# A second-level Strassen product in the first place of the last down projection

## The chip, the cores and the metric

The kernel runs on one core of one Trainium2 chip. The metric is the device time of one execution in microseconds. Before the change the three timed runs took 714.13, 714.17 and 714.49 us; the median is 714.17.

The core has a matrix engine (TensorE, PE in the profile; its weight loads are shown as PEld), a vector engine (VectorE, DVE), a scalar engine (ScalarE, ACT), a general engine (GpSimd, POOL) and a queue for transfers (SyncE, SP). Each takes its own instructions in order, and they wait for each other by semaphores. Matrix products are summed in eight banks of PSUM of 128x512 floats.

## The reference

One transformer block on 2048 tokens with 1024 features, in bfloat16: a layer norm, linear attention with a residual, a second layer norm, and a gated feed-forward net with a residual. What the change touches is the net:

```python
h = x + _A_ref(_layernorm(x, axis=-1), A_wqkv, A_wo)
h2 = h + _B_ref(_layernorm(h, axis=-1), B_W_gate, B_W_up, B_W_down)
# _B_ref:
gate = jnp.einsum("bsd,df->bsf", x, W_gate)
up = jnp.einsum("bsd,df->bsf", x, W_up)
gate = gate * (lambda x, dt: x.astype(dt))(gate > 0, gate.dtype)
h = gate * up
return jnp.einsum("bsf,fd->bsd", h, W_down)
```

W_gate and W_up are 1024x3584, W_down is 3584x1024.

## The kernel before

The net is done in two passes of 1024 tokens. Each pass has 14 feed-forward units (`ffn_unit`, L1660; even ones make gate, odd ones up for four blocks of 128 hidden features) and then a down projection (`down_pass`, L1950). This document is about the second pass: its units run from 471 to 633 us, its down projection from 633 to the end.

The down projection of a pass is a matrix product of 1024 tokens x 3584 hidden features with 3584 x 1024 weights. It is done by the Strassen-Winograd scheme: hidden activations and weights are split into 2x2 blocks, and seven products of blocks or of sums of blocks take the place of eight. The seven are numbered 0 to 6. A product in the **direct** form (`direct`, L2076) is 56 matmuls with 512 columns: 14 pairs of hidden blocks times four groups of 128 tokens, weights brought in five chunks (`WCH`). A product in the **second-level** form (`level2`, L2102) applies the same scheme once more within the product: seven smaller products M1, M7, M6, M2, M5, M4, M3 (in this order) of 14 matmuls with 256 columns each. Each M takes one 448 KB weight operand from the ring `wdring` and one operand of activations. Four of the seven activation operands are sums (`l2_sums`, L1905, on VectorE, L1908), called sg here, one for each of M7, M5, M6 and M3; the other three are quarters of the block. Of the weight operands, too, four are sums.

In the second pass before the change, product 0 is direct and products 1 to 6 are second-level (`L2SET`, L692). A product of the second level uses four banks, `a, f, b, c`: M1 into a, copied by ScalarE into b (a fork, L850); M7 into f; M6 adds to b, which is forked into c; M2 adds to a; M5 adds to c; M4 adds to b; M3 adds to c. So M3 may not start before M5 has been read out of c. Products use the banks 0 to 3 and 4 to 7 in turn.

When an M has been summed, its bank is read into the float buffers U and V or into the output tiles, a quarter at a time (`q_add`, L2004, a VectorE addition from PSUM, 128x512). `ev` adds into U or V; `ev_out` makes an output tile of 128x512 and adds it to the output in memory by a transfer from GpSimd (L1977); M7 is read twice, the others once for each target. Product 4 serves two targets. Product 0 before the change is copied out of PSUM by ScalarE twice: into U (`e_s1`) and, later, into Wf in the tensor RH (`e_w`, L1987), since product 1 adds to U while product 2 needs the first product alone.

The order of VectorE's work in a down pass is written by hand: `at(p, i, f)` puts f behind the i-th unit of product p (L2174 on), and i counts chunks of a direct product or the M's in the order above, from 0. There go the sums sg for the products ahead, D2 (`d2`, L2066; the difference of D1 and a block, an operand of product 1) and D4 (`d4`, L2070; an operand of product 6), each in two instructions of 128x3584. GpSimd adds the residual h of one output block to U (`add_h`, L1994) behind product 3, from a tile that SyncE loads (`ld_h`, L1958).

The weight operands are made once. Those of product 2 are made in the second pass: in each pair of units a raw piece is loaded (`load_xr`, L736), stored to memory as it is, and VectorE makes four differences of 128x256 that are stored too (`x_wsums`, L741). Those of products 1, 3, 4, 5, 6 are made in the first pass (`wl_sums`, L801), where for one of them GpSimd does the subtractions (`addw`, L823 and 824), each of them tied to TensorE's latest instruction and called from `mid`, a list that `ffn_unit` takes from at fixed places (L1817, 1825, 1869, 1880). In the second pass `mid` is empty.

Weights come by a ring of nine buffers in the second pass; the load for a buffer is issued by SyncE as soon as TensorE is done with it.

A unit's products are called P1 to P7, and the M's within P5 and within P1 of the next unit M1 to M7 and R1 to R7; h11, h12, h21, h22 are the four quarters of its result, and c12, c22 and s5a are VectorE's reads out of PSUM (L1707). Behind the last unit `hh_pair` makes D1 and D3.

Of the kernel before, what the change touches and what calls it, by code (L numbers as in the profile page):

```python
# [132 lines left out]
def bass_sequential_preLN__linear_attn_block__glu_gated_reglu__prompt_kernel(  # L133
# [63 lines left out]
    t_v = t_scr.rearrange("p (k o m c) -> p k o m c", k=2, o=8, c=HNW)  # L197
    r_scr = nc.dram_tensor("r_scr", [P, 2 * NPAIR * NW], bf16).ap()
    r_v = r_scr.rearrange("p (s k m c) -> p s k m c", s=2, k=4, c=HNW)
    l_scr = nc.dram_tensor("l_scr", [6 * 4 * P, WDW], f16).ap()  # L200
    l_v = l_scr.rearrange("(o j p) (m c) -> p o j m c", p=P, j=4, c=HNW)
# [3 lines left out]
    with es:  # L205
# [92 lines left out]
        def x2(st):  # L298
# [17 lines left out]
        xr = RW[:, 0:4 * NW].rearrange("p (z k c) -> p z k c", z=2, k=2)  # L316
        lx = RW[:, 4 * NW:8 * NW].bitcast(f16).rearrange("p (z j c) -> p z j c", z=2, j=4)
        xs1 = RX[:, 0:2 * D].bitcast(f16).rearrange("p (j k t) -> p j k t", j=4, k=2)
        g1 = RX[:, 2 * D:4 * D].bitcast(f16).rearrange("p (s j c) -> p s j c", s=2, j=4)
# [5 lines left out]
        sg_g = [RWG[:, x:x + 4 * WDW].bitcast(f16).rearrange("p (j m t) -> p j m t", j=4, t=SHB)  # L325
                for x in (0, NWX * NDC * 2 * P)]
        XSZ = KH * S // 2

# [78 lines left out]
        sl_xw = slots("dxw_", 2)  # L407
        sl_lx = slots("dlx_", 2)
        sl_out = slots("dout_", NOS)
        sl_out2 = slots("dou2_", STB)  # L410
# [72 lines left out]
        B_lx = [bufs("lx%d_" % i, 4) for i in range(2)]  # L483
        B_rscr = [bufs("rscr%d_" % i, NPAIR) for i in range(2)]
        B_hnE = bufs("hnE_", STB)
# [203 lines left out]
        WSRC = [("b", 0, 0), ("t", 1), ("b", 1, 0), ("t", 2), ("t", 0), ("t", 3), ("b", 1, 1)]  # L689
        LIDX = {("t", 0): 0, ("t", 1): 1, ("t", 2): 2, ("t", 3): 3, ("b", 1, 1): 4, ("b", 1, 0): 5}  # L690
        LSRC = [("q", 0, 0), ("s", 2), ("s", 1), ("q", 1, 0), ("s", 0), ("s", 3), ("q", 1, 1)]
        L2SET = [(1, 3, 4, 5, 6), (1, 2, 3, 4, 5, 6)]  # L692
        WLIST = []
        for p2 in range(NPASS):
            for pi, src in enumerate(WSRC):
                if pi in L2SET[p2]:
                    WLIST += [(p2, src, x) for x in LSRC]
                else:
                    WLIST += [(p2, src, c) for c in WCH]
# [11 lines left out]
        def load_wd_next():  # L711
            L = wd_next[0]
            if L >= wd_lim[0]:
                return
            wd_next[0] += 1
            i = wd_slot(L)
            _, src, x = WLIST[L]
            dst = wdring[i]
            if src in LIDX and x[0] in ("s", "q"):
                li = LIDX[src]  # L720
                if x[0] == "s":
                    ap, rd = l_v[:, li, x[1]], B_lscr if li < 4 else B_wscr if li == 4 else B_xscr
                elif li < 4:
                    ap, rd = t_v[:, x[1], 2 * li + x[2]], B_tscr[x[1]::2]
                else:
                    ap, rd = r_v[:, li - 4, 2 * x[1] + x[2]], B_rscr[li - 4][x[1]::2]
                if x[0] == "s" or li < 4:
                    dst = dst.bitcast(f16)
                dma(sl_wd[i], dst.rearrange("p (m c) -> p m c", c=HNW), ap, "ld_wl_%d" % L, reads=rd,
                    writes=[B_wd[i]])  # L730
                return
            q0, q1 = x
            dma(sl_wd[i], dst[:, 0:(q1 - q0) * NW].rearrange("p (q c) -> p q c", c=NW),
                wd_v[:, src[1], q0:q1, src[2] * NW:(src[2] + 1) * NW], "ld_wd_%d" % L, writes=[B_wd[i]])
# [6 lines left out]
        def x_wsums(m):  # L741
# [20 lines left out]
            def two():  # L762
# [3 lines left out]
                load_xr(m + 2)  # L766
            return [one, two]

        def load_wraw(q):
# [889 lines left out]

        def ffn_unit(ps_, n, pre, wina, winb, mid=(), lna=(), lnb=(), tail=()):  # L1660
            Lg = (ps_ * NPAIR + n) * 2
# [164 lines left out]
            else:  # L1826
# [13 lines left out]
                if n == 0:  # L1840
# [6 lines left out]
                dve(ftmp[:, 1, :].rearrange("p (t c) -> p t c", t=2), bank(BE[1]).rearrange("p (t c) -> p t c", t=2),  # L1847
                    m5.unsqueeze(1).to_broadcast([P, 2, SHB]), [B_X, B_s5[0]], [B_s5[1]], "s5a")
                r15()
                p6(1)  # L1850
# [32 lines left out]
            if up:  # L1883
                fin5(1, 1, c22, B_c22, "h22")
                fin5(1, 0, c12, B_c12, "h12")
            else:
# [47 lines left out]

        def sg_hole(t1):
            v = hh16[:, 0:NFT:2, t1 * SBW:(t1 + 1) * SBW]

            def go(j, m0=0, m1=NM):
                b0, c0 = NM * (j // 2), (j % 2) * SHB
                return v[:, b0 + m0:b0 + m1, c0:c0 + SHB], [B_hh[2 * (b0 + m)][t1] for m in range(m0, m1)]  # L1940
            return go

        q_d2 = q_flat(D2, lambda k, m0, m1: [B_D2])
        q_d1 = q_flat(D1, lambda k, m0, m1: [B_D1[2 * m + k] for m in range(m0, m1)])
        q_10, q_11, q_d3, q_d4 = q_hh(1, 0, hh), q_hh(1, 1, hh), q_hh(0, 1, hh16), q_hh(1, 0, hh16)
        sg_ro, sg_rg0, sg_rg2 = sg_plain(sg_o, B_sgo), sg_plain(sg_g[0], B_sgg), sg_plain(sg_g[1], B_sgg)
        sg_x0, sg_x1 = sg_hole(0), sg_hole(1)
        V4 = (ftmp[:, 0:STB], B_U), (ftmp[:, STB:2 * STB], B_V)

        def down_pass(ps_, fill):  # L1950
# [35 lines left out]

            def e_w(j):  # L1987
                ident_act(Wf[:, j], bank(XB[j]), [B_bank[XB[j]]], [B_W[j]], "dsw")

# [112 lines left out]
            def level2(pi, bks, Q, sg, evac, spare=None):  # L2102
# [3 lines left out]
                def prod(mi, bk, x, start):  # L2106
# [3 lines left out]
                    wd_use[0] += 1  # L2110
                    w = wdring[ws]
                    if WSRC[pi][0] == "t" or WLIST[L][2][0] == "s":
                        w = w.bitcast(f16)
# [47 lines left out]
            OS, O2 = (outst, B_outst), (out2, B_out2)  # L2161
            sgs = {1: sg_ro, 2: sg_rg2, 3: sg_x0, 4: sg_ro, 5: sg_rg2 if last else sg_rg0, 6: sg_x1}
            direct(0, XB, a_hh(0, 0), True, e_s1)
            level2(1, YB, q_d2, sgs[1], ev("dU", (U, U)))
            if last:
                level2(2, XB, q_10, sgs[2], ev_out(0, 0, WV, OS, sl_out))
            else:
                direct(2, XB, a_hh(1, 0), False, e_11)
            level2(3, YB, q_d3, sgs[3], ev("dV", (V, U)))
# [21 lines left out]
            hi = (2, 3, 0, 1)  # L2191
            at(0, 0, lambda: d2(0, NH), lambda: d2(NH, NPAIR))
            at(0, 1, sg6[0])
            at(0, 2, *sg6[1:3])
            at(0, 3, sg6[3])
            for i in range(4):
                at(1, 2 + i, sg7[i])
            sg5 = l2_sums(q_d1, sgs[4], "sg5")
            for i in range(4):
                at(2, (1 + i) if not last else 2 + i, sg5[i])  # L2200
            if not last:
                claim(B_sgg, B_w[0:4])
                at(2, 2, lambda: d4(0, NH))
# [3 lines left out]
            else:  # L2207
                claim(B_W, B_hnT)
                at(1, 0, *each(e_w))
                for i in range(4):  # L2210
                    at(3, 2 + i, sg4[i])
                at(2, 0, lambda: ld_h(0, 1))
                at(3, 0, lambda: d4(0, NH))
                at(3, 6, *each(add_h, U, 0, 1, order=hi))
                at(5, 0, lambda: d4(NH, NPAIR))
            for i in range(4):
                at(5, 1 + i, sg3[i])
            for f_, places in fill:
# [278 lines left out]
        for p_ in range(NPASS):  # L2497
            done = []
            for q in range(NPAIR):
# [11 lines left out]
                if p_ == 0:  # L2511
# [25 lines left out]
                    if q == NPAIR - 1:  # L2537
                        for _ in range(NWS - 4):
                            load_wd_next()
                    continue  # L2540
                if q == 0:
                    claim(B_xr + flat(B_lx), B_wd[0:NWS - 3])
                    load_xr(0)
                    load_xr(1)
                if q > 0:
                    winb.append(tq[3])
# [7 lines left out]
                else:  # L2554
                    claim(B_sgg, B_w[2:6])
                    g_ = l2_sums(q_10, sg_rg2, "sg2", 0, NM - 1)
                    winb.append(g_[0])
                if q % 2 == 0:
                    winb.append(w0_)
                ffn_unit(1, q, pre, wina, winb)  # L2560
                if q == NPAIR - 3:
# [3 lines left out]
                if q == NPAIR - 1:  # L2565
                    claim(B_wd[0:NWS - 3], B_xr + flat(B_lx))
                    for _ in range(NWS - 3):
# [11 lines left out]
            else:  # L2579
                claim(B_V, B_xs5 + flat(B_g5))  # L2580
                claim(B_hres + B_ds, B_xs1 + flat(B_g1))
                ge = l2_sums(q_10, sg_rg2, "sg2", NM - 1, NM)
                late = [(g_[1], (0, 3)), (ge[0], (1, 0)), (ge[1], (1, 0)), (g_[2], (1, 1)),
                        (ge[2], (2, 0)), (g_[3], (2, 0)), (ge[3], (2, 0))]
            if p_ + 1 < NPASS:
# [83 lines left out]
```

## Time and profile before

| | us |
|---|---|
| median of three runs | 714.17 |
| the profiled execution | 714.61 |
| its span, first to last instruction | 712.8 |
| TensorE busy | 706.6 |
| VectorE busy | 606.0 |
| ScalarE busy | 411.5 |
| GpSimd busy | 143.1 |
| product 0 of the last down pass (633.04 to 645.12) | 12.08 |
| product 2 of it (655.93 to 666.63) | 10.70 |
| the last weight load on TensorE ends | 709.74 |

The profile is one execution. Engines' times overlap, so what counts is where TensorE has to wait; the chain of work that ended last shows it. In a list of groups or a timeline a line ends with the idle time ahead of the instruction and what ended it, in brackets. TensorE's clock was 1.000 throughout.

### The profile page before, as it was taken

To read this page: it belongs to the slowest core of one execution; us is meant where nothing else is said; L and a number is where in the kernel's file an instruction comes from. 1 tells how busy PE (TensorE), PEld (TensorE's weight loads), DVE (VectorE), ACT (ScalarE), POOL (GpSimd) and SP (SyncE) were. 2 spreads that over 40 slices of the span, in tenths; PEclk is the share of its full clock that TensorE was granted. 3 is DMA by queue.
4 is the path that set the end of the run, shared out by engine and by line. 5 is a ranking of instruction groups with operands and counts; after the bars stand their busy time and mean duration, and the time that the engine had idled before them with its cause. 6 is when DMAs were issued, how large, how long until landed. Compare 5 with 4: busy or idle time off the path is not lost.

```text
span 712.8 us, 13267 instructions
## 1 busy us (share of the span) xinstructions
PE 706.6 (99%) x5039; PEld 391.6 (55%) x5039; DVE 606.0 (85%) x974; ACT 411.5 (58%) x741; POOL 143.1 (20%) x206
## 2 busy tenths in 40 slices
PE   8999999999999999999999999999999999999998
PEld 3344444444444455555554658865555555547887
DVE  6988867899878899999998787888889888988985
ACT  4887666764973687878786411046666767633010
POOL 3231100114982223132312001310000000000331
PEclk9999999999999999999999999999999999999999
DMA  9843244114999799999897989995344544267996
GB/s 297 262 104 77 36 119 164 39 31 95 233 199 287 224 330 290 327 255 297 261 294 239 275 247 319 318 220 159 100 132 114 144 120 125 74 207 256 320 317 187
DMA packets 195104, 144.21 MB, mean 202 GB/s; under 512 B 53984, under 2 KB 172512, under 8 KB 195040
## 3 DMA queue, kind: packets, MB, share of 16 engines
q1 hardware_dynamic: 190048, 138.77, 66.9%
q0 software_dynamic: 4032, 3.67, 3.7%
q10 hardware_dynamic: 960, 0.92, 0.4%
q8 instruction: 40, 0.66, 0.4%
q14 instruction: 24, 0.20, 0.1%
HBM read 98.76 MB, written 32.51 MB: 184 GB/s over the span
## 4 chain that ended last, share of the span: by engine, by line
PE 93%; DMA 2%; DVE 2%; issue 1%; SPq 1%; ACT 0%
PE ps L845 93%; DMA RE<-in_A_x_dram 1%; DMA RAB<-in_A_wqkv_dram 1%; DVE RW L1068 1%; DMA RAB<-RXH 1%; DVE RC L1068 1%; SPq L637 1%; ACT RXH L885 0%; DVE RWG L1093 0%; DVE RE L1968 0%; DVE st L859 0%; DVE RX L1184 0%; DVE RE L1245 0%; DVE RWG L1908 0%; DVE RX L929 0%
## 5 line engine op out<-in xcount | busy, mean ns | idle before, releaser
L850 ACT ACTIVATE ps<-ps 128x512 f32<-128x512 f32 (+1 forms) x263 | 133.1, 517 | 182.2 <-PE ps L845 138.1
L845 PE MATMUL ps<-RC,RO 128*128 128x512 f16 x616 | 147.0, 370 | 0.0
L845 PEld LDWEIGHTS ps<-RC,RO 128*128 128x128 f16 x616 | 59.9, 98 | 53.3 <-ACT ps L850 1.2
L850 ACT ACTIVATE RE<-ps 128x512 f32<-128x512 f32 (+3 forms) x106 | 63.8, 627 | 32.1 <-PE ps L845 18.0
L845 PE MATMUL ps<-RC,RWG 128*128 128x512 f16 x320 | 81.0, 380 | 0.6 <-DVE RC L1068 0.6
L845 PE MATMUL ps<-RH,RWG 128*128 128x512 bf16 (+1 forms) x348 | 77.7, 349 | 0.0
L1977 POOL DMA_DIRECT2D out_dram<-RX x20 | 17.9, 1258 | 271.5 <-DVE RX L1968 218.4
L845 PE MATMUL ps<-RH,RO 128*128 128x512 bf16 (+1 forms) x256 | 65.3, 380 | 0.0
L1707 DVE TENSOR_TENSOR RE<-ps,RE 128x1024 bf16<-128x1024 f32 (+1 forms) x42 | 44.0, 1047 | 18.2 <-PE ps L845 18.1
L845 PE MATMUL ps<-RW,RAB 128*128 128x256 f16 (+3 forms) x374 | 56.0, 304 | 0.0
L845 PEld LDWEIGHTS ps<-RH,RWG 128*128 128x128 bf16 x348 | 33.9, 98 | 35.3 <-ACT ps L850 0.2
L845 PE MATMUL ps<-RAB 128*128 128x512 bf16 (+3 forms) x250 | 52.9, 350 | 0.0
L845 PEld LDWEIGHTS ps<-RC,RWG 128*128 128x128 bf16 (+1 forms) x320 | 29.9, 97 | 35.3 <-ACT ps L850 5.5
L845 PEld LDWEIGHTS ps<-RW,RAB 128*128 128x128 f16 (+1 forms) x374 | 36.3, 98 | 16.2 <-DVE RAB L1419 0.5
L1968 DVE TENSOR_TENSOR RE<-ps,RE 128x512 f32<-128x512 f32 x44 | 30.2, 686 | 14.4 <-PE ps L845 11.8
L1719 ACT ACTIVATE RAB<-RAB 128x1024 bf16<-128x1024 bf16 x28 | 29.5, 1053 | 18.9 <-DVE RAB L1707 18.9
L1707 DVE TENSOR_TENSOR RAB<-ps,RE 128x1024 bf16<-128x1024 f32 x28 | 34.2, 1222 | 7.2 <-PE ps L845 6.5
L1707 DVE TENSOR_TENSOR RAB<-RAB,RE 128x1024 bf16<-128x1024 bf16 x56 | 37.3, 686 | 3.1 <-ACT RE L850 2.8
L1573 DVE TENSOR_TENSOR RO<-RWG 128x1024 f16<-128x1024 bf16 x54 | 39.4, 729 | 0.0
L845 PEld LDWEIGHTS ps<-RH,RO 128*128 128x128 f16 (+1 forms) x256 | 24.3, 98 | 24.7 <-ACT RX L850 1.5
L1573 DVE TENSOR_TENSOR RO<-RWG,RO 128x1024 f16<-128x1024 bf16 x54 | 37.8, 700 | 0.0
L845 PEld LDWEIGHTS ps<-RAB 128*128 128x128 bf16 (+1 forms) x250 | 24.2, 98 | 21.8 <-ACT RAB L988 0.3
(212 smaller groups left out, 1294.0 us busy)
## 6 DMA issues: line engine op xcount, KB each, us to landing
RWG<-in_B_W_gate_dram SPq DMA_DIRECT2D x28, 512.0 KB, 6.0
RWG<-in_B_W_up_dram SPq DMA_DIRECT2D x28, 512.0 KB, 4.9
RW<-l_scr SPq DMA_DIRECT2D x20, 448.0 KB, 5.4
RW<-in_B_W_down_dram SPq DMA_DIRECT2D x14, 512.0 KB, 6.1
t_scr<-RW SPq DMA_DIRECT2D x14, 512.0 KB, 4.3
l_scr<-RX SPq DMA_DIRECT2D x7, 1024.0 KB, 8.8
RE<-l_scr SPq DMA_DIRECT2D x15, 448.0 KB, 5.4
RW<-t_scr SPq DMA_DIRECT2D x13, 448.0 KB, 5.2
```

Of the source, the lines that this page charges most:

```text
L637: return PL.add(eng, lambda e: e.dma_start(dst_ap, src_ap), reads=reads, writes=writes, slot=slot, name=name)
L845: lambda e: e.matmul(out_ap, lhsT, rhs, start=start, stop=stop, skip_group_check=skip),
L850: PL.add("act", lambda e: e.activation(out=dst, in_=src, func=func), reads=reads, writes=writes, name=name)
L1068: PL.add("dve", lambda e: e.tensor_tensor(out=t(j)(d), in0=in0(d), in1=in1(d), op=ALU.subtract), reads=reads, writes=[btw[j]], name="%s%d" ...
L1573: PL.add(eng, lambda e: e.tensor_tensor(out=tb(j, u), in0=f0(u), in1=f1(u), op=ALU.subtract), reads=[B_w[i + x] for x in r] + ([B_T[k + x] ...
L1707: PL.add("dve", lambda e: e.tensor_tensor(out=dst, in0=in0, in1=in1, op=op), reads=reads, writes=writes, name=name)
L1719: PL.add("act", lambda e: e.activation(out=d, in_=d, func=ACTF.Relu), reads=[], writes=db, name=name)
L1968: PL.add(eng, lambda e: e.tensor_tensor(out=dst, in0=in0, in1=in1, op=op), reads=reads, writes=writes, name=name)
L1977: PL.add("pool", lambda e: e.dma_start(dst, src, accum_op=ALU.add), reads=[bsrc], writes=[B_hscr[st]], slot=sl, name="acc_%d_%d" % (st, dh))
```

## The change

In the second pass product 0 becomes a second-level product, and the products go in the order 0, 2, 1, 3, 4, 5, 6.

- Product 0's weight operands are made in the second pass's units: `load_yr` loads a raw piece of 256 KB (seven in all) and stores it; `y_wsums` has GpSimd make four differences of 128x256 for each, tied to TensorE's latest instruction, and stores them. They are taken from `mid`, three per unit, at three places (behind s5a, a new one, and behind P7 and P3), so units 0 to 9 have them.
- Product 0's activation sums (sg0) stand in the last unit and behind it, in pieces over six of the seven m and the last one, five of these pieces in a new list `tail2` ahead of the multiplication h12. The sums of product 2 (sg2) move into product 0, one buffer for each, in RX and RH.
- `ev0` reads product 0 into U: M2, M7 (twice) and M3 by ScalarE, M5 and M4 added by VectorE. The copy into Wf (`e_w`) goes; product 2 reads U before product 1 adds to it, and uses Wf for its middle result.
- D2 goes behind product 0 (its first half) and M1 of product 2. D4 goes in four pieces of 4, 3, 4 and 3 blocks, behind M5 and M3 of product 1, M4 of product 3 and M1 of product 5. The sums of later products move with them; the loads of h go behind M2 of product 2.
- The holes of the activation operand that take the sums of products 3 and 6 are guarded by one buffer per sum instead of one per block.

```diff
-        L2SET = [(1, 3, 4, 5, 6), (1, 2, 3, 4, 5, 6)]
+        ORDER = [list(range(7)), [0, 2, 1, 3, 4, 5, 6]]
+        L2SET = [(1, 3, 4, 5, 6), tuple(range(7))]
...
+        def load_yr(m):
+            if m < NM:
+                z = m % 2
+                dma(sl_yw[z], yr[:, z], wd_v[:, 0, 2 * m:2 * m + 2, 0:NW], "ld_yw_%d" % m, writes=[B_yr[z]])
+                dma(sl_ry[z], r_v[:, 2, :, m, :], yr[:, z].rearrange("p k (h c) -> p (k h) c", c=HNW), "st_ry_%d" % m,
+                    reads=[B_yr[z]], writes=B_rscr[2][2 * m:2 * m + 2])
+
+        def y_wsums(m):
...
+            def add(j, x, y):
+                PL.add("pool", lambda e: e.tensor_tensor(out=ly[:, j, :], in0=x[0], in1=y[0], op=ALU.subtract),
+                       deps=[PL.prog["pe"][-1]], reads=x[1] + y[1], writes=[B_ly[j]], name="WY%d_%d" % (j, m))
+
+            def last():
+                add(3, q_(1, 0), t_(1))
+                dma(sl_ly[0], l_v[:, 6, :, m, :], ly, "st_ly_%d" % m, reads=B_ly, writes=[B_yscr[m]])
+                load_yr(m + 2)
...
                     m5.unsqueeze(1).to_broadcast([P, 2, SHB]), [B_X, B_s5[0]], [B_s5[1]], "s5a")
+                run(mid, 1)
...
                 fin5(1, 1, c22, B_c22, "h22")
+                go(tail2)
                 fin5(1, 0, c12, B_c12, "h12")
...
-            def e_w(j):
-                ident_act(Wf[:, j], bank(XB[j]), [B_bank[XB[j]]], [B_W[j]], "dsw")
+            def ev0(m, b):
+                def cp(T, H):
+                    d, bd = quad(U, T, H)
+                    ident_act(d, qb(b), [B_bank[b]], bd, "ds1")
+                if m == 2:
+                    cp(0, 0)
+                elif m == 7:
+                    cp(1, 1)
+                    cp(1, 0)
+                elif m == 5:
+                    q_add(U, U, 1, 1, b, "dU")
+                elif m == 4:
+                    q_add(U, U, 1, 0, b, "dU")
+                elif m == 3:
+                    cp(0, 1)
...
-            direct(0, XB, a_hh(0, 0), True, e_s1)
-            level2(1, YB, q_d2, sgs[1], ev("dU", (U, U)))
             if last:
-                level2(2, XB, q_10, sgs[2], ev_out(0, 0, WV, OS, sl_out))
+                level2(0, XB, q_00, sgs[0], ev0)
+                level2(2, YB, q_10, sgs[2], ev_out(0, 0, U, OS, sl_out, WV))
+                level2(1, XB, q_d2, sgs[1], ev("dU", (U, U)))
             else:
+                direct(0, XB, a_hh(0, 0), True, e_s1)
+                level2(1, YB, q_d2, sgs[1], ev("dU", (U, U)))
                 direct(2, XB, a_hh(1, 0), False, e_11)
...
-                at(1, 0, *each(e_w))
-                for i in range(4):
-                    at(3, 2 + i, sg4[i])
-                at(2, 0, lambda: ld_h(0, 1))
-                at(3, 0, lambda: d4(0, NH))
+                sg2 = l2_sums(q_10, sgs[2], "sg2")
+
+                D4C = ((0, 4), (4, 7), (7, 11), (11, NPAIR))
+
+                def spread(pi, fs, cs=(3, 4, 5, 6)):
+                    for f_, c_ in zip(fs, cs):
+                        at(pi, c_, f_)
+                spread(0, sg2)
+                at(0, 6, lambda: d2(0, NH))
+                at(2, 0, lambda: d2(NH, NPAIR))
+                spread(2, sg6)
+                spread(3, sg5, (2, 4, 5, 6))
+                for i, c_ in enumerate(((1, 6), (3, 3), (4, 6), (5, 0))):
+                    at(*c_, sg4[i])
+                for i, c_ in enumerate(((1, 4), (1, 6), (3, 5), (5, 0))):
+                    at(*c_, lambda i=i: d4(*D4C[i]))
+                at(2, 3, lambda: ld_h(0, 1))
                 at(3, 6, *each(add_h, U, 0, 1, order=hi))
-                at(5, 0, lambda: d4(NH, NPAIR))
             for i in range(4):
-                at(5, 1 + i, sg3[i])
+                at(*((5, 1 + i) if not last else ((5, 3), (5, 4), (6, 0), (6, 1))[i]), sg3[i])
...
                 if q == 0:
...
+                    load_yr(0)
+                    load_yr(1)
+                    wys = [f_ for m in range(NM) for f_ in y_wsums(m)]
...
                     claim(B_sgg, B_w[2:6])
-                    g_ = l2_sums(q_10, sg_rg2, "sg2", 0, NM - 1)
+                    g_ = l2_sums(q_00, sg_rg2, "sg0", 0, NM - 1)
                     winb.append(g_[0])
+                    ge = l2_sums(q_00, sg_rg2, "sf0", NM - 1, NM)
+                    tail2 = [ge[0], g_[1], ge[1], g_[2], ge[2]]
...
-                ffn_unit(1, q, pre, wina, winb)
+                ffn_unit(1, q, pre, wina, winb, [wys.pop(0) for _ in range(min(3, len(wys)))], tail2=tail2)
```

In this code the variables `sg6`, `sg7`, `sg4` and `sg3` hold the sums of products 1, 3, 5 and 6, and `sg5` those of product 4; `e_s1` and `direct` are still used in the first pass.

## The prediction

> **What bounds the kernel now.** I read the chain of work that ended last first, then the busy time by stretch, the weight loads in order of time, and VectorE beside GpSimd.
>
> ```profile
> PE 706.6 (99%) x5039; PEld 391.6 (55%) x5039; DVE 606.0 (85%) x974; ACT 411.5 (58%) x741; POOL 143.1 (20%) x206
> ...
> PE 93%; DMA 2%; DVE 2%; issue 1%; SPq 1%; ACT 0%
> ```
>
> The end is set by TensorE: from 44 us to the tail at 710 the chain leaves it once, from 673.0 to 676.1, in the last pass. So a change pays for the matmuls it takes away, less what it makes TensorE wait. The last pass, one stretch for each product of the first level (columns: PE, PEld, DVE, ACT, POOL, PEclk, DMA share, GB/s):
>
> ```profile
> 633.04:645.12 12.08, 12.08 (x57) 5.46 (x56) 11.32 (x11) 1.84 (x3) 0.00 (x0) 1.00 0.66 230
> 645.12:655.93 10.81, 10.81 (x100) 9.56 (x99) 8.68 (x14) 4.38 (x9) 0.00 (x0) 1.00 0.85 278
> 655.93:666.63 10.70, 10.70 (x101) 9.56 (x99) 9.47 (x14) 1.16 (x2) 0.00 (x0) 1.00 0.95 334
> 666.63:677.57 10.94, 10.86 (x100) 9.47 (x98) 10.10 (x11) 1.16 (x2) 6.57 (x6) 1.00 1.02 305
> 688.36:699.06 10.70, 10.70 (x101) 9.56 (x99) 10.36 (x13) 1.16 (x2) 3.56 (x4) 1.00 1.02 276
> ```
>
> The first product costs 12.08 us in the direct form, the others 10.7 in the second-level form. The clock is full. VectorE is 9 to 10 us busy of 10.7, and the DMA engines are near full: these are the two covers that could go. Where TensorE's loads wait:
>
> ```profile
> 645.12 1.62 PEld L845 LDWEIGHTS ps<-RW,RC 128*128 128x128 f16 x14
> 646.76 1.52 PEld L845 LDWEIGHTS ps<-RW,RO 128*128 128x128 f16 x14
> ...
> 676.14 1.42 PEld L845 LDWEIGHTS ps<-RWG,RAB 128*128 128x128 f16 x14 [0.35 <-DVE RE L1968]
> ...
> 686.92 1.42 PEld L845 LDWEIGHTS ps<-RW,RO 128*128 128x128 f16 x14 [0.19 <-DVE RE L1968]
> ```
>
> One M (14 matmuls) takes 1.527 us (10.70 / 7 is 1.528); the first after 512-wide matmuls takes 0.11 more. The last M of products 3 and 4 (M3) waits until VectorE has read M5 out of the bank that M3 adds to. Each wait shortens its M by 0.10, so the two cost 0.25 and 0.09 net. VectorE there:
>
> ```profile
> 671.33 1.08 DVE L1908 TENSOR_TENSOR RWG<-RAB 128x1792 f16<-128x1792 bf16 x1
> 673.05 0.69 DVE L1968 TENSOR_TENSOR RE<-ps,RE 128x512 f32<-128x512 f32 x1 [0.64 <-PE ps L845]
> 673.66 1.83 DVE L1908 TENSOR_TENSOR RWG<-RAB 128x1792 f16<-128x1792 bf16 x1
> 675.41 0.68 DVE L1968 TENSOR_TENSOR RE<-ps,RE 128x512 f32<-128x512 f32 x1
> ```
>
> The second sum takes 1.83 instead of 1.08, because GpSimd adds the residual at the same time (from 673.39 to 674.53): the sum ends 0.96 after GpSimd does. Behind it the read of M5 ends at 676.09, and M3 starts at 676.14.
>
> In the last feed-forward pass, 478 to 633, TensorE waits for nobody; VectorE waits for it:
>
> ```profile
> DVE RE L1707 <- PE ps L845: 12.0, 20, 2.0
> DVE RAB L1707 <- PE ps L845: 4.6, 14, 0.9
> ```
>
> That is 16.6 us over 14 units, 1.2 us of slack a unit.
>
> **The change, part by part.**
>
> Product 0 (56 matmuls of 512 columns become 98 of 256): 12.08 becomes 7 x 1.527 = 10.69, so -1.39. The 0.11 moves from product 1 to product 0: 0.
>
> Emptying product 0: four ScalarE copies of 0.6 become four of a half bank each (0.6) and two VectorE adds of 0.69. ScalarE was idle for 9.6 us ahead of the old ones. The first two write where h21 is read, so they wait for it (637.2) and hold the copy of M6's bank behind them until 638.9; M5 wants that at 639.26, margin 0.3. The four copies to RH at 647.56 go; only VectorE waited for them. TensorE: 0.
>
> Operand sums of product 0. Its first part takes the place of the one at 628.47 (0.95, same form). Five more stand ahead of the last h12 multiply: 0.29, 0.95, 0.29, 0.95, 0.29 from 633.54 on (rows of 128x256 and 128x1536), each overlapping its forerunner by 0.08 or, where it reads it, 0.03 after it. They end at 636.0 to 636.1. Who waits: M7 needs the first (633.8, it starts at 634.68), M6 the last, at 633.04 + 1.64 + 1.53 = 636.21. Margin 0.1; I take 0, and for the range 0 to 0.6 (two of the 0.29 rows late). Queued behind them: h12, h21, D1, D3, each some 2.5 later, the last done at 638.4 instead of 636.85. Their readers are now later than before: the sums of product 2, from 639.4. The fourth sum (0.95 + 0.29 after M6) ends at 639.6; M3 wants it at 642.3. The old sums for q_10 go from 645.21 to 658.87 in pieces, to four whole ones of 1.08 in product 0, each in its own buffer, so none waits for a reader.
>
> D2 (2 x 2.02) moves from 636.77 to 645 to 649, behind M3 of product 0 and M1 of product 2; it puts off emptying M7 of product 2 from 647.2 to 649.3, and nobody needs that bank before product 3. D4, 2 x 2.01, becomes four pieces: 1.20, 0.95, 1.20, 0.95 (from 0.95 at 1536 elements and 1.08 at 1792), +0.27 of VectorE. In all VectorE has 4.3 (four sums) + 1.4 + 0.3 = 6.0 us more in a pass of 76.7 with 13.8 idle.
>
> To see what waits, I walked the three queues of the last pass in their new order, with the durations above, 0.08 overlap between VectorE instructions, a bank readable 1.84 after its M's loads began. Done on the old order the walk gives M3 of products 3, 4, 5 waits of 0.44, 0.14, 0.08 (trace 0.35, 0.19, 0) and the last load's end at 709.73 (trace 709.74). The new order, M5 read against M3 due: product 0 641.8 and 642.3; product 2 652.95 and 653.0; product 1 663.25 and 663.7; product 3 674.36 and 674.38; product 4 waits 0.26; product 5 695.4 and 695.85. The last load ends at 708.06. So the wait in product 3 is gone (sums of 1.08 are spread wider and D4 no longer stands ahead of it) and -0.25 comes with it; product 4's stays: 0.
>
> One price there is not in the trace as such: in product 3 a sum waits for GpSimd's first residual add while the second is queued. If VectorE goes next, the walk holds; if GpSimd does, M3 waits 1.23 and the whole saving is 0.6. The nearest case: at 301.39 a VectorE subtraction stood behind a GpSimd add (to 302.00) with another GpSimd instruction next; it came first and took 1.69 instead of 1.21, and GpSimd's next, usually 0.19, took 1.17. So VectorE goes first: 0, other end +1.05.
>
> Weights of product 0 in the feed-forward pass: 28 GpSimd subtractions, 0.67 each (the same form in pass 0: 28 with median 0.67), tied to TensorE's M3, P7 and P3 in units 0 to 9, exactly where VectorE begins a read of PSUM (0.69 or 1.22 long). In pass 0 the 1.22 us reads beside such a subtraction took 1.225 (others 1.209 to 1.225); SBUF-only sums that began under one took 1.16 instead of 0.68. Under their PSUM reads they cost 0; where one slips out, 0.48 of VectorE, out of 1.2 slack. I take 0; the ends are 0 and 28 x 0.67. The Trainium skill (SBUF — State Buffer, Who interferes with whom) has a stricter rule: a VectorE instruction with two SBUF inputs blocks fully against a GpSimd one that reads SBUF. The 1.16 row agrees with it. By a rule of thumb in Perfetto Trace Analysis (Optimizing Scalar/DVE Operations), that moving work between these two engines may not help, the sum would be the upper end of the third rival, 720; by the row of 1.225 it stays 712.6.
>
> SyncE: seven loads and fourteen stores of 256 KB. Each store of raw weights waits for its load's landing (3.1 us by the row of 256 KB loads) and holds the loads of gate and up weights behind it, in the worst unit by 0.67 + 0.9 of issue + 3.1 = 4.7 us. These are issued 8.6 us into a unit and first read two units later, over 14 us on; they land in 3.7 to 6. Cost 0. The x loads behind them are two deep, 23 us apart.
>
> Weight loads in the last pass: 5 of 256 to 384 KB become 7 of 448. At 448 KB per 1.527 us they ask for 300 GB/s; 334 and 361 were moved in products 2 and 4. A slot is needed 12.2 us after its load is issued; the slowest landed in 8.0. Product 0's stretch had a third of the DMA time free. The four residual loads move on SyncE from 658.17 to some 650; the weight load behind them is issued 1.1 us late there as it is now. The accumulating stores of block (0,0), 3.5 us of GpSimd's queue from 666.83, move to 654, so GpSimd's adds no longer stand close behind them. Cost 0.
>
> Sum: -1.39 - 0.25 = -1.64, of which I keep -1.6 for margins of 0.02 to 0.1. The profiled execution took 714.61 (span 712.8 and 1.81 around it), so 713.0; it is 0.44 above the median of the three runs, 714.17, so 712.6.
>
> **Rivals.** A, the sum: 712.3 to 712.9. B, some of VectorE's backlog reaches M3 or M6 (GpSimd first in product 3, or M6 of product 0 late by 0.6 and product 2 by 0.4): saving 0.6, 713.6. For it: margins of 0.02 to 0.1 in the walk. Against: it reproduces the old waits within 0.1. C, slower: GpSimd's 28 subtractions slip off the PSUM reads and VectorE loses its slack in units 0 to 9. 9.3 units have 11.1 us of slack; at 0.48 each the loss is 13.4, so 2.3 reach TensorE: 714.17 - 1.6 + 2.3 = 714.9; at the full 0.67 each, 7.7 reach it: 720. It decides from 0.4 us per subtraction on. For it: 11 of 28 were slowed so in pass 0. Against: those were tied to other places, and TensorE did not wait there either. D, that second-level matmuls do not give 1.39: excluded by six neighbours of 10.7.
>
> **Numbers.** A 0.62, B 0.24, C 0.14. A measurement tells 0.2%, 1.43 us, from no change: A is beyond it but for its upper edge (0.55 faster, 0.07 same), B within (0.24), C mostly beyond (0.12 slower, 0.02 same). Predicted A's 712.6; the range 712.2 to 714.4 takes in B and leaves out most of C.
>
> **What would show it.** Right: the first product's stretch 10.8 us; product 3's M3 loads without a wait; VectorE's s5a, c22 and c12 reads at 0.69 and 1.22 with GpSimd beside them; no TensorE wait before the last pass. Wrong: M6 of product 0 waiting for VectorE; a sum of over 2 us in product 3; SBUF sums of 1.16 in units 0 to 9 and TensorE waiting there.

## The result, and the profile after

The changed kernel took 712.86 us (median of 22 runs, 712.42 to 713.41) beside 714.12 us for the kernel before on the same chip (22 runs, 713.8 to 715.4): 1.26 us less, a ratio of 0.9982 with a 95% interval of 0.9975 to 0.9988. It is faster, but by 0.18%, just inside the 0.2% that the prediction set as the bound of no change. The profiled execution took 712.97 us, of which 711.2 are the span. TensorE's clock was 1.000 throughout.

First the page: TensorE's weight loads and matmuls, the other engines' busy time, and the chain of work that ended last.

```profile
PE 706.0 (99%) x5081; PEld 397.2 (56%) x5081; DVE 611.9 (86%) x982; ACT 410.9 (58%) x739; POOL 162.3 (23%) x234
...
PE 95%; DVE 2%; DMA 1%; ACT 1%; issue 0%
```

There are 42 more matmuls (98 instead of 56 in product 0), VectorE is 5.9 us busier and GpSimd 19.2, and TensorE carries the end as before. Next the last pass by product, in the new order 0, 2, 1, 3, 4 (columns as before: PE, PEld, DVE, ACT, POOL, PEclk, DMA share, GB/s).

```profile
632.76:643.69 10.93, 10.93 (x100) 9.49 (x99) 10.62 (x17) 3.88 (x6) 0.00 (x0) 1.00 0.91 320
643.69:654.51 10.82, 10.82 (x101) 9.51 (x98) 10.72 (x12) 1.76 (x3) 0.00 (x0) 1.00 0.89 301
654.51:665.21 10.70, 10.70 (x101) 9.59 (x99) 9.29 (x12) 1.16 (x2) 3.56 (x4) 1.00 1.06 318
665.21:675.91 10.70, 10.70 (x101) 9.54 (x99) 10.67 (x14) 1.16 (x2) 3.89 (x2) 1.00 1.01 377
675.91:686.77 10.86, 10.86 (x101) 9.51 (x99) 10.46 (x15) 1.16 (x2) 3.13 (x3) 1.00 0.88 306
```

Product 0 fell from 12.08 to 10.93 and product 3 from 10.94 to 10.70. But product 2 costs 10.82 and product 4 10.86 where 10.70 is the price without a wait. VectorE is 10.5 to 10.7 us busy in four of these five stretches. The weight loads show where TensorE stood:

```profile
632.76 1.62 PEld L886 LDWEIGHTS ps<-RE,RAB 128*128 128x128 bf16 x14
634.39 1.52 PEld L886 LDWEIGHTS ps<-RE,RWG 128*128 128x128 f16 x14
636.13 1.44 PEld L886 LDWEIGHTS ps<-RAB,RWG 128*128 128x128 f16 x14 [0.22 <-issue]
...
653.06 1.44 PEld L886 LDWEIGHTS ps<-RW,RH 128*128 128x128 f16 x14 [0.21 <-issue]
...
674.43 1.46 PEld L886 LDWEIGHTS ps<-RE,RAB 128*128 128x128 f16 x14
...
685.32 1.44 PEld L886 LDWEIGHTS ps<-RWG,RO 128*128 128x128 f16 x14 [0.25 <-issue]
```

("issue" means that the profile names nobody who released it.) M3 of product 3 (674.43) has lost its wait. M6 of product 0 (636.13) and M3 of product 2 (653.06) have gained one each, and M3 of product 4 (685.32) waits 0.25 instead of 0.19. Behind a wait the 14 loads take 1.44 instead of 1.52, so the three cost about 0.13, 0.13 and 0.17 net.

From here on a pass is measured in the trace, from product 0's first weight load to the program's last instruction: before 633.04 to 712.82, that is 79.78; after 632.76 to 711.23, that is 78.47. The 1.31 between them is 1.39 (product 0) + 0.25 (wait of product 3) - 0.13 - 0.13 - 0.08 (product 4, from 0.09 to 0.17 net) = 1.30. The pass is used because the program's beginning varies: the pass starts anywhere from 632.5 to 633.8 in the profiled executions of kernels in which TensorE waits for nobody in the units, and that shift is there when unit 0 begins; the units' period of 11.69 us repeats to 0.01. So a tenth of a microsecond can be read within the pass, and not in run times.

### The profile page after: what moved, and what is told of

The parts are those of the page before. It is cut to its first block, busy times and chain, and to the rows that moved or that the text cites. A ratio compares the mean times of both kernels' runs of the same rounds, so it can differ in the third digit from the quotient of the medians.

```text
span 711.2 us, 13434 instructions
## 1 busy us (share of the span) xinstructions
PE 706.0 (99%) x5081; PEld 397.2 (56%) x5081; DVE 611.9 (86%) x982; ACT 410.9 (58%) x739; POOL 162.3 (23%) x234
## 4 chain that ended last, share of the span: by engine, by line
PE 95%; DVE 2%; DMA 1%; ACT 1%; issue 0%
PE ps L886 95%; DMA RAB<-RXH 1%; DVE RC L1109 1%; DVE RW L1109 0%; DMA RE<-in_A_x_dram 0%; DVE RWG L1134 0%; ACT RXH L926 0%; PE ps L1047 0%; DVE st L900 0%; DVE RX L1225 0%; DVE RE L1286 0%; PE ps L1026 0%; DVE RH L1134 0%; DVE RX L970 0%; DVE RXH L1011 0%
## 5 line engine op out<-in xcount | busy, mean ns | idle before, releaser
L886 PE MATMUL ps<-RW,RAB 128*128 128x256 f16 (+3 forms) x354 | 51.8, 299 | 0.0
L886 PE MATMUL ps<-RAB 128*128 128x512 bf16 (+3 forms) x238 | 50.1, 348 | 0.0
L886 PEld LDWEIGHTS ps<-RW,RAB 128*128 128x128 f16 (+1 forms) x354 | 34.5, 98 | 13.8 <-DVE RAB L1460 0.5
L800 POOL TENSOR_TENSOR RW<-RW 128x256 f16<-128x256 bf16 x28 | 18.7, 669 | 89.4 <-PE ps L886 67.2
```

The source lines that it names most:

```text
L800: PL.add("pool", lambda e: e.tensor_tensor(out=ly[:, j, :], in0=x[0], in1=y[0], op=ALU.subtract), deps=[PL.prog["pe"][-1]], reads=x[1] + y ...
L886: lambda e: e.matmul(out_ap, lhsT, rhs, start=start, stop=stop, skip_group_check=skip),
```

## The experiments

**1. Product 0 direct in the new order.** Is the saving the second level's, or the order's and the buffers'?

```diff
-        L2SET = [(1, 3, 4, 5, 6), tuple(range(7))]
+        L2SET = [(1, 3, 4, 5, 6), (1, 2, 3, 4, 5, 6)]
-                level2(0, XB, q_00, sgs[0], ev0)
+                direct(0, XB, a_hh(0, 0), True, e_s1)
...
-                spread(0, sg2)
-                at(0, 6, lambda: d2(0, NH))
+                spread(0, sg2, (1, 2, 3, 4))
+                at(0, 4, lambda: d2(0, NH))
```

Product 0's weight work in the units and its sums go with it.

> The new product order, D4 in four pieces and one buffer per sum stay; product 0 is direct again, and neither its weight operands nor its activation sums are made. Theory (terms): product 0's stretch is 12.08 us again, the wait of M3 in product 3 stays gone (-0.25 against the kernel before), product 2's wait goes too since VectorE has 6 us less to do; so about 0.2 us faster than the kernel before (ratio 0.9997) and 1.05 us slower than the changed one. Rival (the gain is from order and pieces, not from the second level): within 0.3 us of the changed kernel, ratio 0.9985 or below.

It took 714.14 us, a ratio to before of 0.9996 (0.9987 to 1.0005). The pass took 79.61. Its weight loads at M3 of products 3 and 4:

```profile
675.60 1.47 PEld L886 LDWEIGHTS ps<-RWG,RAB 128*128 128x128 f16 x14
686.49 1.44 PEld L886 LDWEIGHTS ps<-RW,RO 128*128 128x128 f16 x14 [0.25 <-issue]
```

The wait of product 3 is gone with the new order and places alone, and the one of product 4 is there at its new size: 0.17 less than before (0.25 - 0.08). No wait is left in product 2. The second level itself brings 79.61 - 78.47 = 1.14, which is 1.39 less the two waits of 0.13 that come with it, in product 0 and in product 2.

**2. The weight work taken away.** Product 0 reads product 6's weight operands in place of its own, so the loads, the 28 GpSimd subtractions and the stores in the units go, and the part of the result that depends on product 0 is not the reference's.

```diff
-        LIDX = {("b", 0, 0): 6, ("t", 0): 0, ("t", 1): 1, ("t", 2): 2, ("t", 3): 3, ("b", 1, 1): 4, ("b", 1, 0): 5}
+        LIDX = {("b", 0, 0): 4, ("t", 0): 0, ("t", 1): 1, ("t", 2): 2, ("t", 3): 3, ("b", 1, 1): 4, ("b", 1, 0): 5}
-                    load_yr(0)
-                    load_yr(1)
-                    wys = [f_ for m in range(NM) for f_ in y_wsums(m)]
+                    wys = []
```

> The changed kernel without the making of product 0's weight operands: no loads and stores of raw pieces, no GpSimd subtractions; product 0 reads product 6's weight operands in their place, so this part of the result is left out. Theory (the subtractions cost TensorE nothing): the last feed-forward pass has the same length within 0.1 us, VectorE is busy 1.1 us less there, and the time is that of the changed kernel within 0.1 us (ratio to the kernel before 0.998). Rival (GpSimd, SyncE or the transfers cost time there): 0.3 us or more faster than the changed kernel, ratio 0.9977 or below.

713.04 us, ratio 0.9981 (0.9972 to 0.999), pass 78.48 with the same three waits. The work in the units costs TensorE nothing. What it costs VectorE is seen in VectorE's waits for TensorE from 478 to 633 us. The changed kernel:

```profile
DVE RE L1748 <- PE ps L886: 11.1, 20, 2.0
...
DVE RAB L1748 <- PE ps L886: 4.4, 14, 0.9
```

and this experiment:

```profile
DVE RE L1748 <- PE ps L886: 12.0, 20, 2.0
...
DVE RAB L1748 <- PE ps L886: 4.6, 14, 0.9
```

Without the subtractions VectorE has its 16.6 us of slack as before; with them 15.5. All 28 together take 1.1.

**3. The subtractions untied.** They run as soon as their piece has landed, wherever VectorE then is.

```diff
-                       deps=[PL.prog["pe"][-1]], reads=x[1] + y[1], writes=[B_ly[j]], name="WY%d_%d" % (j, m))
+                       reads=x[1] + y[1], writes=[B_ly[j]], name="WY%d_%d" % (j, m))
```

> The changed kernel, but GpSimd's 28 subtractions no longer wait for TensorE's M3, P7 and P3; they run as soon as their data are there. Theory (VectorE has 1.1 us of slack a unit, and only sums within SBUF suffer): some 15 of 28 meet such a sum and stretch it by about 0.45, VectorE is busy 6 us more in units 0 to 9, and TensorE loses 0 to 0.5 us; ratio 0.998 to 0.999. Rival (the third rival of the prediction: the ties are what keeps the change from being slower): 2 us or more lost, ratio 1.001 or above, with TensorE waiting in the units.

713.37 us, ratio 0.9985 (0.9977 to 0.9994). They ran in seven bursts of four. Nine of the 28, not the fifteen expected, met a VectorE sum within SBUF (a sum of 677 ns took up to 1149, others of 418 took 883 to 887), instead of the two that do in the changed kernel. TensorE's waits in the units:

```profile
PEld ps L886 <- DVE RAB L1748: 0.8, 2, 0.4
```

Two waits of 0.4 lengthened two units by 0.12 and 0.06; the pass took 78.47. So the place does count, and its price is 0.2 us: of the nine hits, most fell into slack. By run times this kernel can't be told from the changed one.

**4. The subtractions on VectorE.** The third rival asked what happens when VectorE loses time in the units.

```diff
-                PL.add("pool", lambda e: e.tensor_tensor(out=ly[:, j, :], in0=x[0], in1=y[0], op=ALU.subtract),
-                       deps=[PL.prog["pe"][-1]], reads=x[1] + y[1], writes=[B_ly[j]], name="WY%d_%d" % (j, m))
+                PL.add("dve", lambda e: e.tensor_tensor(out=ly[:, j, :], in0=x[0], in1=y[0], op=ALU.subtract),
+                       reads=x[1] + y[1], writes=[B_ly[j]], name="WY%d_%d" % (j, m))
```

> The changed kernel with the 28 subtractions for product 0's weight operands on VectorE instead of GpSimd, at the same places in its order. Theory (VectorE has slack, it waits for TensorE 15.5 us from 478 to 633): 28 x 0.29 = 8.1 us more VectorE work, its waits for TensorE fall to about 8, units 0 to 9 stay at 11.69 us each (TensorE loses 0 to 0.3 us in all). Rival (the slack does not lie where it is needed: two of three places stand right ahead of a read that TensorE's P4 waits for): units lengthen by 0.1 us or more each, 1 us or more in all.

A single run: 714.74 us (the kernel before beside it: median 714.39). Its pass was 78.46, so the loss is ahead of it. The stretch from unit 0 to the last unit in this kernel, then in the changed one:

```profile
473.74:624.38 150.64, 150.08 (x869) 84.50 (x868) 134.25 (x258) 98.27 (x190) 0.00 (x0) 1.00 0.56 159
```

```profile
473.23:622.60 149.37, 149.37 (x870) 84.89 (x869) 131.14 (x230) 98.63 (x190) 18.72 (x28) 1.00 0.57 161
```

It is 1.27 longer with VectorE only 3.1 busier (134.25 against 131.14; the 28 take 0.28 each, but busy time counts neighbours that overlap once). TensorE waited, from 470 to 633:

```profile
PEld ps L886 <- ACT ps L891: 1.4, 5, 0.4
PEld ps L886 <- DVE RAB L1748: 1.0, 1, 1.0
PEld ps L886 <- DVE RE L1748: 0.2, 1, 0.2
```

Two of the five waits for ScalarE, 0.5 in all, lie at 472 us, ahead of unit 0, and the changed kernel has them too. VectorE still had 10.7 us of slack (its waits for TensorE), so it isn't the sum of its work that reached TensorE. Unit 0 lost 0.66 of the 1.27, units 1, 3 and 7 0.16 to 0.23. VectorE stood 2.7 us for the landings and stores of the raw pieces, and the subtractions lie ahead of reads that TensorE wants. How much is due to the one and how much to the other was not separated.

**5. D4 in two instructions.** Was it D4 that had to leave product 3?

```diff
-                D4C = ((0, 4), (4, 7), (7, 11), (11, NPAIR))
+                D4C = ((0, NH), (NH, NPAIR))
-                for i, c_ in enumerate(((1, 4), (1, 6), (3, 5), (5, 0))):
+                for i, c_ in enumerate(((3, 0), (5, 0))):
```

> The changed kernel with D4 in two pieces of 128x3584 behind M1 of product 3 and M1 of product 5, as before the change. Theory (the wait of M3 in product 3 depends on who is first at the port, VectorE's sum or GpSimd's residual add, not on D4): it stays gone or nearly so (under 0.1), the last pass is as long as the changed kernel's within 0.1 us, 78.47 from its first weight load to the end. Rival (D4 in four pieces removed the wait, as the prediction said): M3 of product 3 waits 0.35 again and the pass is 0.25 us longer.

A single run: 713.4 us, pass 78.50. VectorE in product 3, then the loads of M3 in products 3 and 5:

```profile
667.73 2.02 DVE L2015 TENSOR_TENSOR RAB<-RAB,RC 128x3584 f16<-128x3584 bf16 x1
...
674.77 1.52 PEld L886 LDWEIGHTS ps<-RE,RAB 128*128 128x128 f16 x14
...
696.45 1.44 PEld L886 LDWEIGHTS ps<-RW,RWG 128*128 128x128 f16 x14
```

Product 3 has no wait, though the first half of D4 (2.02) now stands in it again. The three waits of the changed kernel stay (0.21, 0.21, 0.25). One is new: M3 of product 5, behind the second half of D4, starts 0.12 late. By the pass the four pieces are worth 0.03 us.

**6. The residual addition left out of the kernel before.** From the kernel before, GpSimd's four additions of the residual (two of them in product 3) and the loads for them are taken away; one output block lacks its residual.

```diff
-                at(2, 0, lambda: ld_h(0, 1))
...
-                at(3, 6, *each(add_h, U, 0, 1, order=hi))
```

> The kernel before without GpSimd's four residual adds of the last output block and their loads, so that block lacks its residual. Theory (the sum that GpSimd holds up for 0.75 us is the cause of the wait): the second sum of product 3 takes 1.08 instead of 1.83, M3 of product 3 does not wait, the last pass is 0.25 us shorter, 79.53 from its first weight load to the end. Rival (VectorE's own backlog in product 3 is the cause): M3 waits 0.2 us or more as before.

A single run: 714.0 us. VectorE in product 3:

```profile
673.37 1.08 DVE L1908 TENSOR_TENSOR RWG<-RAB 128x1792 f16<-128x1792 bf16 x1
674.37 0.68 DVE L1968 TENSOR_TENSOR RE<-ps,RE 128x512 f32<-128x512 f32 x1
```

The sum that took 1.83 takes 1.08, the read of M5 is early, and M3 does not wait; the wait of 0.19 in product 4 stays. The pass is 79.52, 0.26 less than before. So without GpSimd's additions the wait of product 3 is not there, with D4 and all of VectorE's own work in place.

**7 and 8. The waits moved.** If the new waits are sums that come too late, placing those sums elsewhere removes them. The first of the two:

```diff
-                spread(2, sg6)
+                spread(2, sg6[:3], (4, 5, 6))
+                at(1, 0, sg6[3])
-                for i, c_ in enumerate(((1, 4), (1, 6), (3, 5), (5, 0))):
+                for i, c_ in enumerate(((1, 4), (1, 6), (4, 6), (5, 2))):
-                at(*((5, 1 + i) if not last else ((5, 3), (5, 4), (6, 0), (6, 1))[i]), sg3[i])
+                at(*((5, 1 + i) if not last else ((5, 4), (5, 6), (6, 0), (6, 1))[i]), sg3[i])
-                    tail2 = [ge[0], g_[1], ge[1], g_[2], ge[2]]
+                    tail2 = [ge[0], ge[1], g_[2], ge[2]]
+                    wys = [lambda: None, lambda: None, g_[1]]
```

One 0.95 us piece of product 0's sums goes into the last unit, one sum of product 1 leaves product 2, the last two pieces of D4 go behind M3 of product 4 and M6 of product 5, and the first two sums of product 6 follow them.

> The changed kernel with three of VectorE's places moved: the second piece of product 0's sums into the idle time ahead of the read c12; the sums of product 1 one M later; D4's last two pieces behind M3 of product 4 and M6 of product 5, and product 6's first two sums later. Theory (three waits by VectorE's backlog cost 0.13 in M6 of product 0, 0.13 in M3 of product 2, 0.08 to 0.17 in M3 of product 4): the first two waits are gone, the third is 0.14 instead of 0.25; the last pass is 0.3 us shorter, ratio to the kernel before 0.9978. Rival (these waits have another cause, the label of their releaser being unknown): they stay, and the time is that of the changed kernel.

712.76 us, ratio 0.9981 (0.9972 to 0.999), pass 78.30. M6 of product 0 and M3 of product 2 no longer wait. Product 4 still waits 0.25, where less was expected, and a new wait of 0.15 stands ahead of M6 of product 6: the sum put behind product 6's M1 ends at 701.41, and M6 begins at 701.48. The second of the two puts that sum one product earlier:

```diff
-                at(*((5, 1 + i) if not last else ((5, 4), (5, 6), (6, 0), (6, 1))[i]), sg3[i])
+                at(*((5, 1 + i) if not last else ((5, 4), (5, 5), (5, 6), (6, 1))[i]), sg3[i])
```

> As the run with three places moved, but product 6's sums stand behind M5, M4 and M3 of product 5, where VectorE was idle, instead of M5, M3 and M1 of product 6. Theory (each remaining wait is one place in VectorE's queue): the wait of M6 in product 6 that the move had made (0.15) is gone, no new one comes, only product 4's 0.25 is left; the last pass is 78.15 to 78.25 from its first weight load to the end, against 78.47 in the changed kernel, ratio to the kernel before 0.9977 to 0.9980. Rival (the work only moves on and another M waits): 78.3 or more.

712.84 us, ratio 0.9981 (0.9972 to 0.999), pass 78.22. Product 0's M6, product 2's M3, and product 4's M3 in it:

```profile
636.29 1.52 PEld L886 LDWEIGHTS ps<-RAB,RWG 128*128 128x128 f16 x14
...
653.11 1.52 PEld L886 LDWEIGHTS ps<-RW,RH 128*128 128x128 f16 x14
...
685.44 1.44 PEld L886 LDWEIGHTS ps<-RWG,RO 128*128 128x128 f16 x14 [0.25 <-issue]
```

One wait is left. Against the changed kernel the pass is 0.25 shorter, as two waits of 0.13 ask for; in the run times, whose medians are 0.02 apart, that can't be told. So it is the best version here by its trace only.

## Why the prediction was right, and where its steps were not

The time, 712.86, lies within the likeliest case (712.3 to 712.9) and the range. The saving came out at 1.31 in the trace and 1.26 in the medians, where 1.6 was kept. By the bound of 0.2% it falls into "same", though: the case's upper edge, to which 0.07 was given. That it lies inside the likeliest case, by 0.04, is partly luck: the saving that was kept was 0.3 too large, and the median of the kernel before was 714.12 to 714.40 in the three sets of runs.

**Product 0's matmuls: right.** Experiment 1 against the changed kernel gives 1.14, and with the two waits of 0.13 that come with it 1.40, for 1.39.

**Operand sums ahead of M6 of product 0: mis-sized.** The step let them "end at 636.0 to 636.1", with M6 due at 636.21, took a margin of 0.1 as 0 and kept 0.6 as an end. The wait was 0.22, net 0.13. VectorE there, in the changed kernel:

```profile
632.66 0.68 DVE L1748 TENSOR_TENSOR RAB<-RAB,RE 128x1024 bf16<-128x1024 bf16 x1
633.26 1.48 DVE L1951 TENSOR_TENSOR RWG<-RAB 128x256 f16<-128x256 bf16 x3
634.77 1.28 DVE L1951 TENSOR_TENSOR RWG<-RWG,RAB 128x1536 f16<-128x1536 f16 x2
635.97 1.28 DVE L1748 TENSOR_TENSOR RAB<-RAB,RE 128x1024 bf16<-128x1024 bf16 x2
```

The last of the five ends at 636.06, M6 was due at 635.92 and started at 636.13. The durations were as forecast (0.29 and 0.95). The gaps weren't: three of the five start 0.03 to 0.04 after their forerunner ends, and only the others overlap it by 0.08. Those three wait for their forerunner, since they read its result or go on writing its buffer. The prediction named both figures and used too many overlaps; each that is missing costs 0.11. With the right gaps its own rows give an end at 636.33 against 636.21.

**M3 of product 2: mis-sized, within VectorE's own stretch.** The walk had the read of M5 at 652.95 for M3 due at 653.0. In the changed kernel, whose pass began 0.28 earlier, that read ends at 652.95 too, 0.28 late by the walk; M3 was due at 652.86 and waited 0.21. The late sums of product 0 did not reach it through VectorE's queue. VectorE, ahead of its read of product 0's M5 and at the read in question; then that first read in experiment 8:

```profile
639.82 1.09 DVE L1951 TENSOR_TENSOR RX<-RAB 128x1792 f16<-128x1792 bf16 x1
641.01 0.69 DVE L2015 TENSOR_TENSOR RE<-ps,RE 128x512 f32<-128x512 f32 x1
...
652.26 0.68 DVE L2015 TENSOR_TENSOR RX<-ps,RH 128x512 bf16<-128x512 f32 x1
```

```profile
641.26 0.69 DVE L2015 TENSOR_TENSOR RE<-ps,RE 128x512 f32<-128x512 f32 x1 [0.71 <-PE ps L886]
```

VectorE was done at 640.91 and idle for 0.10 before it read M5, and in experiment 8, where a piece of 0.95 is gone from ahead of it, it waits 0.71 for TensorE there. So the backlog ended at 641.01. What went on was the delay of TensorE itself, which puts off M3 (0.14 against the walk) about as much as the read (0.18). From 641.01 to 652.95 VectorE has no idle time: 11.94 us, where the walk's two dates (641.8 less a read of 0.69, and 652.95) leave about 11.84. Three of the eleven neighbours there start 0.03 after their forerunner instead of overlapping it; how many of them the walk had is not on record. So the read is 0.09 late instead of 0.05 early, and from its end to the load another 0.12 pass. Experiments 7 and 8 take one sum out of this stretch, and the wait is gone; experiment 1 has none either.

**Product 3: the saving right, its reason half right.** The 0.25 came. The prediction gave two reasons: D4 no longer ahead, which experiment 5 rules out, and sums spread wider. But the sum in question starts at the same place in both kernels, 7.03 us into the product before and 7.06 after. What moved is the other side, GpSimd's additions, and what decided is who came first to what the two engines share, which the prediction had only as a price. GpSimd in product 3 before, then GpSimd and VectorE in the changed kernel:

```profile
671.49 3.04 POOL L1968 TENSOR_TENSOR RE<-RE,RX 128x512 f32<-128x512 f32 x2 [1.13 <-DVE RE L1968]
```

```profile
670.84 3.89 POOL L2015 TENSOR_TENSOR RE<-RE,RX 128x512 f32<-128x512 f32 x2 [10.13 <-DVE RE L2015]
```

```profile
670.67 1.08 DVE L1951 TENSOR_TENSOR RO<-RXH 128x1792 f16<-128x1792 f16 x1
671.67 0.69 DVE L2015 TENSOR_TENSOR RE<-ps,RE 128x512 f32<-128x512 f32 x1
672.27 1.45 DVE L1951 TENSOR_TENSOR RWG<-RAB 128x1792 f16<-128x1792 bf16 x1
673.64 0.68 DVE L2015 TENSOR_TENSOR RE<-ps,RE 128x512 f32<-128x512 f32 x1
674.24 1.44 DVE L1951 TENSOR_TENSOR RO<-RXH 128x1792 f16<-128x1792 f16 x1
```

GpSimd's first addition ran from 670.84 to 672.77, its second to 674.73. The sum at 672.27 began 0.50 before the first addition ended, and ended at 673.72; the second addition then took 1.99, and the sum at 674.24 stood behind it in turn. They alternate. Each sum costs 0.37 more than its 1.08, and the read of M5 still ends at 674.32, before M3 is due at 674.38. Before the change the additions began 0.77 earlier in the product (4.86 us into it, not 5.63), because the reads of M7 that release them ended 0.76 earlier. So the second was under way, from 673.39 to 674.53, when the sum came at 673.66; the sum stood behind all that was left of it, 0.87: 1.83. So the sums that are spread wider do count, but in another way than the prediction said: two of them and a piece of D4 stand ahead of M7's reads and put off GpSimd's additions. This is read off the traces; no run moved the additions alone. "If VectorE goes next, the walk holds" was right, so the other end of +1.05 did not come.

**Product 4: "stays" was right for VectorE and missed TensorE's side.** The walk's 0.26 met the trace's 0.25, but not for its reason. In both kernels the read of M5 ended 0.13 after M3 was due (686.87 for 686.74 before, 685.20 for 685.08 after). But the load started 0.05 after the read before, and 0.12 after it now. Between them lies an instruction of TensorE's queue that only waits for a semaphore (685.24 to 685.29). The kernel's `emit` (L118) gives an instruction with more than one wait such an extra one; before the change M3 of product 4 had none in front. Products 2 and 3 have it ahead of M3 too; in product 3 it goes with a load that starts 0.05 late though the read was in time. Which two semaphores they are the trace doesn't show, and no run took it away: its part in the delay is argued, not shown.

**GpSimd's subtractions: right.** They cost TensorE 0 (experiment 2), and rival C did not come.

```profile
L800 POOL TENSOR_TENSOR RW<-RW x28: 663/669/673, 478.0 to 580.3; 128x256 f16<-128x256 bf16 x28
```

All 28 took their 0.67 (least, median and greatest in ns). Two slipped off the PSUM reads, each the first of its raw piece: it had to wait until the store had emptied the one result buffer. One of the two, GpSimd first, then VectorE:

```profile
505.21 0.67 POOL L800 TENSOR_TENSOR RW<-RW 128x256 f16<-128x256 bf16 x1 [2.43 <-DMA l_scr<-RW]
```

```profile
505.31 1.12 DVE L1614 TENSOR_TENSOR RO<-RWG,RO 128x1024 f16<-128x1024 bf16 x1
```

The sum took 1.12 instead of 0.68. At 551.99 the other took 1.14. So two of 28 cost 0.45 each, a long way from the 0.4 for every one at which rival C decides, and the reads of PSUM beside the others took their usual time (691 to 692 and 1224 to 1225 ns). The two rules that the prediction weighed: by the Trainium skill (SBUF — State Buffer, Who interferes with whom) a VectorE instruction with at most one SBUF input does not meet GpSimd at the port (outside the two-port modes), one with two meets it and the later one blocks, and the order of issue decides who. Each of these was seen here: 1.22 us reads unchanged, sums of 1.12, and the turns taken in product 3. The same skill's doubt in Perfetto Trace Analysis (Optimizing Scalar/DVE Operations) that moving work between the two may not help did not hold: on GpSimd, in these places, it costs TensorE nothing, and on VectorE 1.27 us (experiment 4).

**The rest, costed at 0: right in its effect.** No transfer was waited for in the pass, and TensorE waited for nobody in the units. One date was wrong: the accumulating stores of block (0,0) start at 657.15, not 654. They are in GpSimd's queue behind a wait for the loads of the same tokens' residual; nobody needs them.

**Rival B** named the right places (M6 of product 0 and product 2) at 0.6 and 0.4; they came at 0.13 each, a quarter of the sum, which leaves the saving at 1.3 and not 0.6.

## What to carry to other kernels

When a walk of a queue ends with margins of 0.05 to 0.1 us, they are no reason for 0: go through each pair of neighbours and ask whether the second depends on the first, and whether the waiting instruction has a second semaphore. Work added to GpSimd can be free where it is tied to moments at which VectorE reads PSUM; look for what makes it slip from there, here a single buffer that a store has to empty. Where two engines block each other, ask also when the other one's work is released: here that moved by 0.77 us and took a wait away. A question of 0.1 us is settled by the distance between two instructions within a pass, since runs of one kernel differ by ten times as much.

## What the runs showed of the hardware that was not expected

- VectorE's neighbours overlap by 0.08 us, but where the second waits for the first (because it reads or goes on writing what that wrote) it starts 0.03 to 0.04 after it (the pairs from 632.7 to 653 us): 0.11 us a pair. Three such pairs ahead of product 0's M6 made a wait of TensorE out of a margin of 0.1.
- Between VectorE and GpSimd the one that is already waiting goes next, ahead of an instruction that comes later on the other engine: in product 3 they take turns (1.93 and 1.99 us on GpSimd, 1.45 and 1.44 on VectorE). Each loses 0.12 to 0.13 less than what the other has left when it comes: a sum that meets 0.50 of an addition loses 0.37, one that meets 0.87 loses 0.75.
- Ahead of M3 in products 2, 3 and 4 an instruction of 51 ns on TensorE's queue only waits for a semaphore, and these loads start 0.11 to 0.12 us after VectorE's read. Without it, in products 3 and 4 before the change, it was 0.05. M6 of product 0 has one too, which had been waiting since 634.09, and its load starts 0.07 after the sum.
- The group of 14 loads after a wait is shorter by 0.08 to 0.1 us (1.42 to 1.44 instead of 1.52), so a wait of 0.2 costs 0.13.
